# A new opening list for an attention-and-gate kernel; two lower parts of U are made by TensorE and ScalarE

## The chip, the cores and the metric

The kernel runs on one core of a Trainium2 chip. The metric is device time in microseconds (us), lower is better: the median of three runs, and one profiled execution that shows where the time goes.

The core has five engines that work side by side, each through its own instructions in order: TensorE (PE; its weight loads, PEld, are listed apart), VectorE (DVE), ScalarE (ACT), GpSimd (POOL) and SyncE (SP), which here issues most of the DMA transfers. Matrix products go to PSUM, which has eight banks.

## The reference

```python
a = exp(phi - max(phi, axis=2))                    # phi: 8 batches, 8 heads, 576 rows, 32 memories
a = a / (sum(a, axis=2) + 1e-9)
k_m = einsum('bhsm,bhsd->bhmd', a, k)              # d = 64
v_m = einsum('bhsm,bhsd->bhmd', a, v)
s = q @ k_m.T / 8
attn = exp(s - max(s)); attn = attn / (sum(attn) + 1e-9)
x = (attn @ v_m)                                   # to 4608 tokens x 512
gate = sigmoid(x @ w_gate); val = x @ w_val        # 512 x 1536 each
out = (gate * val) @ w_out                         # 1536 x 512
```

The gate weights and the output weights arrive as 64-bit floats and are made into 32-bit ones by integer operations in the kernel.

## The kernel before

Products that must be exact to about 32 bits are made of three products in a rounded format: every operand is split into an upper part (hi, a rounded copy, made by ScalarE) and a lower part (lo, the rest, a subtraction on VectorE by `rest`, L150). x is never formed: U = v_m x [w_gate, w_val] is made for each batch and each pair of the 12 column tiles f, and then attention (`at`) times U gives gate and value at once.

The work goes in steps (batch b, tile f), 96 in all. The first four batches go through f 0 to 3, then 4 to 7, then 8 to 11; the others through all twelve at a time. A step has two halves c (256 and 320 tokens). A half is: 12 products into one or two banks (`G`), sigmoid on ScalarE (`sg`), product on VectorE (`gm`), hi on ScalarE (`gh`), lo on VectorE (`gl`), and some halves later six products with the output weights (`O`). Beside these run the attention pieces of later batches and the conversion of weights (`CONVERT`: at which step which piece).

The first eight steps, and all loads and preparations ahead of them, are written out by hand in a list, `OPENING`, a word for each piece of work. Each word is recorded in turn, and each of the engines PE, DVE, ACT and POOL keeps the list's order; the transfers keep their order on the queue that issues them. The words that matter here:

- loads (all on SP's queue): `phi b`, `kvm b g` and `kvt b` (keys and values), `q b c`, `gate f` (gate weights of tile f, into the wg area that tiles 4 to 11 will fill later), `out f` (output weights); `more`: the next weights of the conversion table, on POOL's queue before;
- batch b's memories: `amax`, `aexp` (exponential of phi), `T`, `A`, `Z` (turn by TensorE, copy, sum), `K`, `B`, `t`, `V` (keys and values, copies and turns);
- batch b's attention, in halves for b 0: `S` (scores), `tr` (VectorE turns them), `mx`, `ex`, `nm` (softmax), `tn` (turn back), `hi`, `lo` (the two parts of `at`). For b 1 and 2 `tn` writes into the tile named q, which the next batch's q needs;
- weights: `sz` and `bt` (magnitude on ScalarE, four operations on VectorE) for a gate piece; `ws`, `wb`, `wh`, `wl` for output weights;
- `U b f` (eight 32-bit products into two banks, which the trace shows as 16 rows), `uh`, `ul` (hi and lo);
- `E` (the sums of a finished turn, copied to a row and sent away), `W n`: n products on the identity that nothing reads.

`turn_lo` also sends both parts of `at` to memory, for use in later turns, as soon as they are there.

Of the kernel before, what the change touches and what calls it, by code (L numbers as in the profile page):

```python
# [54 lines left out]
A 0 1; q 0 0; sz 2; q 0 1; A 0 0; W 23; K 0 0; bt 2; sz 1; bt 1; W 28; K 0 1; B 0; kvt 1; kvm 1 0;  # L55
kvm 1 1; amax 1; W 5; t 0; V 0 0; V 0 1; W 2; S 0 0; aexp 1; U 0 0; tr 0 0; mx 0 0; S 0 1; uh 0 0;
T 1 1; T 1 0; Z 1; A 1 1; T 1 2; ul 0 0; phi 2; A 1 0; q 1 0; A 1 2; out 3; ex 0 0; tr 0 1; q 1 1; W 7;
K 1 0; out 2; nm 0 0; kvm 2 0; mx 0 1; W 8; K 1 1; B 1; kvm 2 1; tn 0 0; kvt 2; amax 2; ex 0 1; W 5;
t 1; hi 0 0; V 1 0; nm 0 1; aexp 2; W 6; S 1 0; V 1 1; W 5; T 2 2; lo 0 0; T 2 1; A 2 2; S 1 1; tn 0 1;
A 2 1; G 0 0 0; Z 2; hi 0 1; tr 1 0; lo 0 1; T 2 0; tr 1 1; U 0 2; sg 0 0 0; mx 1; A 2 0; G 0 0 1;  # L60
uh 0 2; sg 0 0 1; G 0 1 0; gm 0 0 1; gm 0 0 0; ul 0 2; K 2 0; ex 1; G 0 1 1; gh 0 0 0; nm 1; K 2 1;
sg 0 1 0; gh 0 0 1; G 0 2 0; B 2; kvt 3; out 1; gm 0 1 0; gl 0 0 0; gh 0 1 0; U 1 0; gl 0 0 1;
sg 0 1 1; gl 0 1 0; sg 0 2 0; gm 0 1 1; G 0 2 1; uh 1 0; gm 0 2 0; tn 1; gh 0 1 1; t 2; sg 0 2 1;
ul 1 0; G 0 3 0; hi 1; gm 0 2 1; V 2 0; O 0 0 0; lo 1; ws 1; V 2 1; G 0 3 1; gl 0 1 1; q 2 1; gh 0 2 0;
wb 1; phi 3; sg 0 3 0; kvm 3 0; q 2 0; O 0 0 1; gl 0 2 0; wh 1; gm 0 3 0; G 1 0 0; sg 0 3 1; wl 1;
gh 0 2 1; gm 0 3 1; ws 2; gl 0 2 1; O 0 1 0; sg 1 0 0; wb 2; more; G 1 0 1; gh 0 3 0; gm 1 0 0; wh 2;
gl 0 3 0; amax 3; U 1 2; sg 1 0 1; O 0 1 1; uh 1 2; wl 2; gm 1 0 1; ws 3; ul 1 2; S 2 0; O 0 2 0;
tr 2 0; aexp 3; wb 3; S 2 1; G 1 1 0; gh 0 3 1; tr 2 1; gh 1 0 0; O 0 2 1; wh 3; gl 0 3 1; gl 1 0 0;
# [9 lines left out]
def attn_moe_kernel(  # L78
# [97 lines left out]
    def words_tile(room):  # L176

        if len(wos) == 1:
            return pools["conv"].tile([P, 512, 2], I32, name="words", bufs=room)
        if not late_words:  # L180
            q = att([P, NKT * S], "q").bitcast(I32)
            late_words.append(pools["conv"].tile([P, 512, 2], I32, name="words"))
            late_words.extend(q[:, o : o + 1024].rearrange("p (n t) -> p n t", t=2) for o in (0, 1024))
        late_words.append(late_words.pop(0))
        return late_words[-1]
# [820 lines left out]
```

## Time and profile before

| | |
|---|---|
| median of three runs | 754.13 us (752.48 to 754.15) |
| profiled execution | 754.74 us, span 753.0 us |
| instructions | 13818 |
| busy, PE / PEld / DVE / ACT / POOL | 729.6 / 609.9 / 432.4 / 337.7 / 13.7 us |
| moved by DMA | 93.17 MB |

The span is the time from the first to the last instruction of the program; some two microseconds of the execution lie around it. A line of the timeline names start, length, engine, line, operation, output and inputs, shapes, and in brackets the engine's idle time before it and what ended that. "PE busy" counts the W products too, so that the opening looks fuller than it is.

### The profile page before, as it was taken

The numbers are of one execution on the slowest core, as the hardware profiler recorded it, in microseconds if no ns is written. First come the engines' busy times: TensorE is split into PE (matmuls) and PEld (weight loads), VectorE is DVE, ScalarE is ACT, GpSimd is POOL, SyncE is SP. The second block draws the span as 40 slices with busy tenths as digits, with TensorE's granted clock in tenths as the row PEclk, the third lists the DMA queues.
The fourth block names the chain that finished last, engine by engine and source line by source line (L and its number), as shares of the span: only waits on it lengthen the run. The fifth ranks groups of instructions, "written<-read, shape, count | busy, mean of one in ns | idle before, by whom it ended". The sixth has DMA issues, their size and how long they took to land.

```text
span 753.0 us, 13818 instructions
## 1 busy us (share of the span) xinstructions
PE 729.6 (97%) x5651; PEld 609.9 (81%) x5651; DVE 432.4 (57%) x824; ACT 337.7 (45%) x784; POOL 13.7 (2%) x30
## 2 busy tenths in 40 slices
PE   7998999989999999999999999999999999999997
PEld 5676787868889888878888798887887888888886
DVE  7898656986678854447537634356245643343332
ACT  4387545647444433335434443355333533343331
POOL 0000000011000000000000000000000000000000
PEclk9899899999999999999999999999999999999999
DMA  9977255658557544432344104011000000010002
GB/s 360 360 301 286 86 210 186 232 191 295 188 188 246 182 143 146 161 124 66 134 136 163 64 1 172 1 57 64 2 2 29 29 1 15 1 57 1 1 1 70
DMA packets 30655, 93.17 MB, mean 124 GB/s; under 512 B 3456, under 2 KB 4480, under 8 KB 28032
## 3 DMA queue, kind: packets, MB, share of 16 engines
q1 hardware_dynamic: 22528, 71.31, 26.2%
q0 software_dynamic: 3456, 12.58, 5.0%
q10 hardware_dynamic: 4608, 8.39, 3.3%
q8 instruction: 44, 0.72, 0.4%
q14 instruction: 19, 0.16, 0.1%
HBM read 69.73 MB, written 22.54 MB: 123 GB/s over the span
## 4 chain that ended last, share of the span: by engine, by line
PE 87%; DMA 5%; DVE 4%; ACT 2%; issue 1%; SPq 1%; ACTq 0%; DVEq 0%
PE pu_t L160 52%; PE acc L160 36%; DMA kvm<-in_kvm_dram 2%; DMA q<-in_qT_dram 2%; DMA words<-in_wgv_dram 1%; SPq L146 1%; DMA out_dram<-row 1%; ACT L135 1%; ACT ph L135 0%; ACT sg L135 0%; DVE u_lo L150 0%; ACT at_hi L523 0%; DVE g_lo L150 0%; DVE wg L248 0%; DVE at_lo L150 0%
## 5 line engine op out<-in xcount | busy, mean ns | idle before, releaser
L160 PE MATMUL pu_t<-at_hi,u_hi 128*128 128x256 f32 (+1 forms) x760 | 226.9, 299 | 1.1 <-ACT sg L135 1.1
L160 PE MATMUL pu_t<-at_lo,u_hi 128*128 128x256 f32 (+1 forms) x760 | 223.3, 294 | 0.0
L160 PE MATMUL pu_t<-at_hi,u_lo 128*128 128x256 f32 (+1 forms) x760 | 223.0, 293 | 0.0
L638 DVE TENSOR_TENSOR sg<-pu_t,sg 128x256 f32<-128x256 f32 (+1 forms) x190 | 86.3, 455 | 171.7 <-ACT sg L135 106.5
L135 ACT ACTIVATE sg<-pu_t 128x256 f32<-128x256 f32 (+1 forms) x190 | 78.2, 412 | 188.3 <-PE pu_t L160 180.7
L160 PE MATMUL acc<-wo_hi,g_hi 128*128 128x512 f32 x384 | 154.7, 403 | 0.0
L160 PE MATMUL acc<-wo_hi,g_lo 128*128 128x512 f32 x384 | 151.5, 394 | 0.0
L160 PEld LDWEIGHTS pu_t<-at_hi,u_hi 128*128 128x128 f32 x760 | 142.8, 188 | 10.5 <-issue 2.4
L160 PE MATMUL acc<-wo_lo,g_hi 128*128 128x512 f32 x384 | 151.1, 394 | 0.0
L160 PEld LDWEIGHTS pu_t<-at_lo,u_hi 128*128 128x128 f32 x760 | 142.8, 188 | 5.3
L160 PEld LDWEIGHTS pu_t<-at_hi,u_lo 128*128 128x128 f32 x760 | 142.6, 188 | 0.0
L649 ACT CAST g_hi<-sg 128x256 fp32r<-128x256 f32 x192 | 77.9, 406 | 113.1 <-DVE sg L638 101.8
L150 DVE TENSOR_TENSOR g_lo<-sg,g_hi 128x256 fp32r<-128x256 f32 x192 | 80.4, 420 | 58.2 <-ACT g_hi L649 58.2
L160 PEld LDWEIGHTS acc<-wo_hi,g_hi 128*128 128x128 f32 x384 | 72.2, 188 | 30.7 <-issue 20.9
L160 PEld LDWEIGHTS acc<-wo_hi,g_lo 128*128 128x128 f32 x384 | 72.4, 189 | 17.2
L160 PEld LDWEIGHTS acc<-wo_lo,g_hi 128*128 128x128 f32 x384 | 72.4, 188 | 9.6
L150 DVE TENSOR_TENSOR u_lo<-pu_t,u_hi 128x512 fp32r<-128x512 f32 x93 | 58.3, 683 | 24.7 <-ACT u_hi L569 24.6
L569 ACT CAST u_hi<-pu_t 128x512 fp32r<-128x512 f32 x93 | 48.1, 598 | 27.1 <-PE pu_t L160 27.0
L160 PE MATMUL pu_t<-wg,vT 64*32 64x512 f32 x744 | 49.3, 596 | 3.1 <-DVE wg L248 2.3
L160 PEld LDWEIGHTS pu_t<-wg,vT 64*32 64x32 f32 x744 | 11.4, 105 | 26.0 <-issue 16.6
L135 ACT ACT_TABLE_LOAD x20 | 25.7, 1283 | 2.8 <-DVE g_lo L150 1.8
L689 DVE TENSOR_TENSOR row<-acc,row 128x512 f32<-128x512 f32 x32 | 22.0, 688 | 5.5 <-DMA row<-part 5.5
(110 smaller groups left out, 587.5 us busy)
## 6 DMA issues: line engine op xcount, KB each, us to landing
kvm<-in_kvm_dram SPq DMA_DIRECT2D x16, 1024.0 KB, 8.8
q<-in_qT_dram SPq DMA_DIRECT2D x16, 512.0 KB, 5.4
part<-row SPq DMA_DIRECT2D x32, 256.0 KB, 2.1
row<-part ACTq DMA_DIRECT2D x32, 256.0 KB, 4.5
out_dram<-row SPq DMA_DIRECT2D x32, 256.0 KB, 2.1
words<-in_wgv_dram POOLq DMA_DIRECT2D x10, 512.0 KB, 4.6
ph<-in_phiT_dram SPq DMA_DIRECT2D x8, 576.0 KB, 5.1
at_hi<-at SPq DMA_DIRECT2D x8, 576.0 KB, 4.6
```

Source lines behind the costliest of these rows:

```text
L135: last_act[0] = nc.scalar.activation(*args, **kw)
L146: last_move[queue] = queues[queue].dma_start(dst, src)
L150: return nc.vector.tensor_tensor(lo, x, hi.bitcast(F32), op=ALU.subtract)
L160: last_pe[0] = do(*args, **kw)
L569: nc.scalar.copy(U[b, fs[0]][0][:, r, :nf], pb[r])
L638: last_prod[0] = nc.vector.tensor_tensor(sg, val, sg, op=ALU.mult)
L649: nc.scalar.copy(ghi, prod[:, : 2 * P])
L689: nc.vector.tensor_tensor(st, o, st, op=ALU.add)
```

## The change

The whole opening list is new, and with it some pieces of work are cut more finely or given to another engine:

- Gates 2, 1 and 0 are loaded first, in that order, then converted; gate 3 and all output weights come much later. There are 103 W products in place of 155.
- `bt` is cut in two words (`bc` clamps, `bt` sets the bits), likewise `wb` (`wc`, `wb`), `mx` (`mx`, `ms`) and `nm` (`nz`, `nm`).
- For U 0 0 and U 0 2 the lower part is no longer a subtraction on VectorE. A matrix `minus` (the identity times -1) is multiplied with hi into the same two banks, the eight products of U are added once more (`um`), and ScalarE copies what remains (`u_rest`).
- U 2 2 moves from the tenth step into the list.
- `at` of batches 0 to 2 is sent away by words of their own (`keep`), and the finished rows too (`row`); copies of finished sums of batches 0 to 3 are all ScalarE's (half were VectorE's).
- Gate pieces of the conversion table are 1024 columns wide (512 before), at most two pieces wait at a time, `more` uses SP's queue, and the first conversion comes at step 9 in place of 10. `normalize` and `turn` of later batches are recorded behind the gate work, and the slots in which pieces of later batches come are other ones.

```diff
-out 0; phi 0; gate 0; gate 3; gate 2; kvm 0 0; kvt 0; gate 1; kvm 0 1; ws 0; wb 0; amax 0; wh 0; wl 0;
-sz 0 0; sz 0 1; bt 0 0; aexp 0; bt 0 1; sz 3; W 42; T 0 0; T 0 2; T 0 1; Z 0; A 0 2; bt 3; phi 1;
...
+kvt 0; gate 2; phi 0; gate 1; kvm 0 0; gate 0; kvm 0 1; sz 2; bc 2; amax 0; bt 2; sz 1; aexp 0; bc 1;
+bt 1; W 56; T 0 2; T 0 0; A 0 2; T 0 1; A 0 0; phi 1; sz 0 1; K 0 0; q 0 0; A 0 1; bc 0 1; q 0 1;
+sz 0 0; kvm 1 0; Z 0; bc 0 0; W 3; K 0 1; bt 0 1; B 0; kvt 1; kvm 1 1; amax 1; W 5; t 0; V 0 0; bt 0 0;
...
-    10: [(4, 0)], 11: [(4, 1)], 12: [(5, 0), (5, 1)], 13: [(6, 0), (6, 1)], 14: [(4, 2), (7, 0)], 15: [(7, 1), (5, 2)],
+    9: [(4, 0)], 10: [(5, 0)], 12: [(6, 0)], 13: [(4, 2)], 14: [(7, 0)], 15: [(5, 2)], 16: [(6, 2)], 18: [(7, 2)],
...
+BY_PE = [(0, 0), (0, 2)]
...
-        halves_of[b] = halves_of.get(b, 0) + (2 if c is None else 1)
-        if b < QUAD and halves_of[b] == 2:
-            kept[b] = [dram.tile([P, 2 * S], F32, name=f"at{b}_{i}") for i in range(2)]
-            for d, a in zip(kept[b], at[b]):
-                move(d, a.rearrange("p r n -> p (r n)").bitcast(F32))
+        if QUAD > b >= 3:
+            put_by(b)
...
+    def u_minus(b, fs):
+        pb, hi = loaded[b, "u", fs[0]], U[b, fs[0]][0]
+        for r in range(2):
+            matmul(pb[r], minus, hi[:, r, : len(fs)], start=True, stop=False)
+        u_sum(b, fs, pb, False)
+    def u_rest(b, fs):
+        pb, nf = loaded.pop((b, "u", fs[0])), len(fs)
+        hi, lo = U[b, fs[0]]
+        for r in range(2):
+            last_u[0] = nc.scalar.copy(lo[:, r, :nf], pb[r])
...
-            elif t % 2:
+            elif t % 2 or b < QUAD:
                 nc.scalar.copy(st, o)
...
+    minus = pools["conv"].tile([P, P], F32R, name="minus", bufs=1)
+    nc.scalar.activation(minus, ident, AF.Copy, scale=-1.0)
...
-        begin[2, 0]: ([3, 3, 2, 2, 2, 1], remember(3, True), score(3), attend(3)),
-        begin[0, TURN]: ([2, 2, 1, 1, 1, 1, 1], remember(4)),
+        begin[2, 0]: ([3, 2, 2, 2, 2, 1, 1], remember(3, True), score(3), attend(3)),
+        begin[0, TURN]: ([2, 1, 1, 1, 1, 1, 1, 1], remember(4)),
...
-        sides[begin[b, 0]] = ([1] * 23, score(b + 1, then), attend(b + 1))
+        sides[begin[b, 0]] = (([1] * 6 + [0] * 2) * 3, score(b + 1, then), attend(b + 1))
...
-        if i == DONE + 1:
-            make_u(b, [2, 3])
```

How the rows of the built program move, at three places. First the head of SP's queue, the transfers that everything waits for at the start (words: output weights; wg: gate weights; ph: phi). Before:

```order
L146 DMA words<-in_wo_dram 128x1024
L146 DMA ph<-in_phiT_dram 128x1152
L146 DMA wg<-in_wgv_dram 128x2048 x3
L146 DMA kvm_126<-in_kvm_dram 128x2048
L146 DMA kvt<-in_kvt_dram 128x512
L146 DMA wg<-in_wgv_dram 128x2048
L146 DMA kvm_131<-in_kvm_dram 128x2048
L146 DMA ph<-in_phiT_dram 128x1152
L146 DMA q<-in_qT_dram 128x1024 x2
L146 DMA q<-in_qT_dram 128x256
```

Now:

```order
L146 DMA kvt<-in_kvt_dram 128x512
L146 DMA wg<-in_wgv_dram 128x2048
L146 DMA ph<-in_phiT_dram 128x1152
L146 DMA wg<-in_wgv_dram 128x2048
L146 DMA kvm_127<-in_kvm_dram 128x2048
L146 DMA wg<-in_wgv_dram 128x2048
L146 DMA kvm_130<-in_kvm_dram 128x2048
L146 DMA ph<-in_phiT_dram 128x1152
L146 DMA q<-in_qT_dram 128x1024 x2
L146 DMA q<-in_qT_dram 128x256
```

The output weights are gone from the head, three gates stand there in place of four, and kvt is first.

Second, VectorE from the lower part of batch 0's first half of `at` (at_lo from u_hi, which serves as a room for the turn there) on. Before, the second half's turn and batch 1's scores follow, and then the softmax of batch 1 and the first gate products:

```order
L150 TENSOR_TENSOR at_lo<-u_hi,at_hi 128x2x256
L516 STREAM_TRANSPOSE u_lo<-e 128x320 x2
L364 TENSOR_SCALAR z<-z 128x2
L365 RECIPROCAL rz<-z 128x2
L467 STREAM_TRANSPOSE e<-pu_t 128x256 x2
L150 TENSOR_TENSOR at_lo<-u_lo,at_hi 128x2x320
L467 STREAM_TRANSPOSE e<-acc_577 128x320
L467 STREAM_TRANSPOSE e<-pu_t 128x320
L476 TENSOR_REDUCE mx<-e 128x36
L477 TENSOR_TENSOR e<-e,mx 128x1152
L638 TENSOR_TENSOR sg<-acc_653,sg 128x320
L638 TENSOR_TENSOR sg<-pu_t,sg 128x256
```

Now batch 1's scores come at once, the gate products are mixed with the conversion of gate 3 (wg, 1024 columns):

```order
L150 TENSOR_TENSOR at_lo<-u_hi,at_hi 128x2x256
L478 STREAM_TRANSPOSE e<-acc_509 128x256
L478 STREAM_TRANSPOSE e<-acc_510 128x256
L150 TENSOR_TENSOR at_lo<-u_lo,at_hi 128x2x320
L478 STREAM_TRANSPOSE e<-acc_527 128x320
L478 STREAM_TRANSPOSE e<-pu_t 128x320
L246 TENSOR_SCALAR wg<-wg 128x1024
L247 TENSOR_SCALAR wg<-wg 128x1024
L682 TENSOR_TENSOR sg<-pu_t,sg 128x256
L254 SCALAR_TENSOR_TENSOR wg<-wg 128x1024
L257 SCALAR_TENSOR_TENSOR wg<-wg 128x1024
L682 TENSOR_TENSOR sg<-acc_581,sg 128x320
```

The turn and the sums of phi stand ahead of this piece now, and gate 3's four operations have come into it; the softmax of batch 1 is further down.

Third, SP's queue around the loads of batch 2's q and batch 3's phi. Before (the first row is batch 0's `at` going out, the next at rows batch 1's; q 2 1 comes in two pieces, q 2 0 is the last row):

```order
L146 DMA at_1_620<-at_lo 128x1152
L146 DMA kvt<-in_kvt_dram 128x512
L146 DMA words<-in_wo_dram 128x1024
L146 DMA at_0_858<-at_hi 128x1152
L146 DMA at_1_859<-at_lo 128x1152
L146 DMA q<-in_qT_dram 128x1024
L146 DMA q<-in_qT_dram 128x256
L146 DMA ph<-in_phiT_dram 128x1152
L146 DMA kvm_894<-in_kvm_dram 128x2048
L146 DMA q<-in_qT_dram 128x1024
```

Now (q 2 0 is the fourth row, q 2 1 the two after the gate words):

```order
L146 DMA kvm_690<-in_kvm_dram 128x2048
L146 DMA at_0_694<-at_hi 128x1152
L146 DMA at_1_695<-at_lo 128x1152
L146 DMA q<-in_qT_dram 128x1024
L146 DMA words<-in_wo_dram 128x1024
L146 DMA ph<-in_phiT_dram 128x1152
L146 DMA words<-in_wgv_dram 128x2048
L146 DMA q<-in_qT_dram 128x1024
L146 DMA q<-in_qT_dram 128x256
L146 DMA kvm_949<-in_kvm_dram 128x2048
```

q 2 0 goes ahead of out 3, phi 3 and the gate words, q 2 1 behind them; batch 1's `at` is further down.

More of the change, by code (lines that the diff above doesn't have):

```diff
@@ L54 @@
-sz 0 0; sz 0 1; bt 0 0; aexp 0; bt 0 1; sz 3; W 42; T 0 0; T 0 2; T 0 1; Z 0; A 0 2; bt 3; phi 1;
[L55 to L68, printed above, removed]
@@ new lines @@
+bt 1; W 56; T 0 2; T 0 0; A 0 2; T 0 1; A 0 0; phi 1; sz 0 1; K 0 0; q 0 0; A 0 1; bc 0 1; q 0 1;
+sz 0 0; kvm 1 0; Z 0; bc 0 0; W 3; K 0 1; bt 0 1; B 0; kvt 1; kvm 1 1; amax 1; W 5; t 0; V 0 0; bt 0 0;
+V 0 1; W 2; S 0 0; aexp 1; S 0 1; tr 0 0; U 0 0; mx 0 0; tr 0 1; T 1 1; uh 0 0; T 1 2; T 1 0; ms 0 0;
+phi 2; A 1 0; um 0 0; Z 1; q 1 1; ex 0 0; mx 0 1; A 1 2; nz 0 0; A 1 1; K 1 0; ul 0 0; ms 0 1; K 1 1;
+nm 0 0; ex 0 1; amax 2; B 1; kvt 2; q 1 0; nz 0 1; W 5; t 1; gate 3; aexp 2; kvm 2 1; out 0; tn 0 0;
@@ new lines @@
+nz 1; O 0 0 0; sg 0 2 1; V 2 1; gm 0 2 1; O 0 0 1; sg 0 3 0; nm 1; gh 0 2 0; wh 1; G 0 3 1; gh 0 2 1;
+gl 0 2 0; wl 1; tn 1; ws 2; O 0 1 0; sg 0 3 1; gm 0 3 0; hi 1; gm 0 3 1; U 1 2; wc 2; gh 0 3 0;
+O 0 1 1; lo 1; uh 1 2; ul 1 2; G 1 0 0; q 2 0; gh 0 3 1; out 3; phi 3; gl 0 3 0; more 0; wb 2; G 1 0 1;
+q 2 1; kvm 3 1; gl 0 3 1; wh 2; gl 0 2 1; G 1 1 0; wl 2; sg 1 0 0; sg 1 0 1; gm 1 0 0; ws 3; gm 1 0 1;
+O 0 2 0; sg 1 1 0; wc 3; gm 1 1 0; wb 3; G 1 1 1; gh 1 0 0; gl 1 0 0; wh 3; amax 3; S 2 0; sg 1 1 1;
@@ new lines @@
+O 0 2 1; gm 1 1 1; tr 2 0; S 2 1; wl 3; aexp 3; U 2 0; tr 2 1; O 0 3 0; mx 2; uh 2 0; G 1 2 0;
+gh 1 0 1; ms 2; E 0 3 0 0; gh 1 1 0; row 0 0; O 0 3 1; ul 2 0; E 0 3 0 1; ex 2; row 0 1; gl 1 1 0;
+G 1 2 1; gl 1 0 1; gh 1 1 1; nz 2; E 0 3 1 0; E 0 3 1 1; O 1 0 0; row 1 1; gl 1 1 1; kvt 3; nm 2;
+G 1 3 0; sg 1 2 0; sg 1 2 1; gm 1 2 0; gm 1 2 1; O 1 0 1; gh 1 2 0; tn 2; sg 1 3 0; G 1 3 1; gh 1 2 1;
+gm 1 3 0; gl 1 2 0; hi 2; gl 1 2 1; O 1 1 0; sg 1 3 1; lo 2; U 2 2; gm 1 3 1; gh 1 3 0; q 3 1;
+gl 1 3 0; keep 1; O 1 1 1; more 1; uh 2 2; row 1 0; q 3 0; ul 2 2; keep 2; gh 1 3 1; O 1 2 0; gl 1 3 1;
@@ L174, in attn_moe_kernel, with words_tile @@
     late_words = []
-    def words_tile(room):
+    def words_tile(k):
         if len(wos) == 1:
[L179 to L185, printed above, removed]
+            words = pools["conv"].tile([P, 1024, 2], I32, name="words", bufs=2)
+        elif k == 2:
+            words = pools["conv"].tile([P, 512, 2], I32, name="words")
+        else:
+            if not late_words:
+                late_words.append(att([P, NKT * S], "q").bitcast(I32)[:, :2048].rearrange("p (n t) -> p n t", t=2))
+            words = late_words[0]
+        return words[:, :512] if k == 2 else words
     def load_jobs(n=None, queue="stream"):
@@ L199, in load_jobs @@
             n = n and n - 1
+    early_out = []
     def load_out(f):
-        words = words_tile(WORDS[0])
+        if not early_out:
+            early_out.extend(pools["conv"].tile([P, 1024, 2], I32, name="words", bufs=2) for _ in range(2))
+        words = words_of[f, 2] = early_out[f // 2][:, f % 2 * 512 : f % 2 * 512 + 512]
         move(words.rearrange("p n t -> p (n t)"), wo[f].bitcast(I32))
-        words_of[f, 2] = words
-        waiting.append((f, 2))
     def target(f, k):
@@ L244, in bits_of @@
         )
+    def bits_of(dst, words):
+        low, high, bits = words[:, :, 0], words[:, :, 1], dst.bitcast(I32)
         nc.vector.scalar_tensor_tensor(
@@ L694, in out_end, with out_put @@
                 nc.vector.tensor_copy(st, o)
-            if f == NFT - 1:
-                move(out[b * S + t * P : b * S + (t + 1) * P, :], st)
-            else:
-                part[b, t] = dram.tile([P, DM], F32, name=f"part{b}_{t}_{f}")
-                move(part[b, t], st)
+            stored[b, t] = st
+            if put:
+                out_put(b, f, t)
+    stored = {}
+    def out_put(b, f, t):
+        st = stored.pop((b, t))
+        if f == NFT - 1:
+            move(out[b * S + t * P : b * S + (t + 1) * P, :], st)
+        else:
+            part[b, t] = dram.tile([P, DM], F32, name=f"part{b}_{t}_{f}")
+            move(part[b, t], st)
     rows = {}
@@ L856, in attend @@
     def attend(b):
-        normalize(b)
+        with behind():
+            normalize(b)
         yield
-        turn(b)
+        with behind():
+            turn(b)
         if b + 1 < B and b + 1 != QUAD:
```

78 lines of the change are left out of this document (51 added, 27 removed), and 3 rows, old and new, of the table CONVERT.

## The prediction, made before the changed kernel was run

> **What bounds the kernel now.** I read the busy shares first, then what TensorE waits for, then the busy times stage by stage, then the start of the trace in order of time.
>
> ```profile
> PE 729.6 (97%) x5651; PEld 609.9 (81%) x5651; DVE 432.4 (57%) x824; ACT 337.7 (45%) x784; POOL 13.7 (2%) x30
> ...
> PE pu_t L160 <- DMA q<-in_qT_dram: 4.2, 1, 4.2
> ...
> PE pu_t L160 <- DVE wg L248: 2.3, 2, 1.8
> PE pu_t L160 <- ACT ph L135: 1.8, 1, 1.8
> ```
>
> TensorE is busy 97% of the span, so time can only come from where it is idle, or busy with nothing. Its longest waits are a load of q, one of keys and values (4.0, its row is below), two on converted gate weights, one on an exponential. The stages show the rest (columns: length; busy us of PE, weight loads, DVE, ACT, POOL; granted clock; DMA share; GB/s):
>
> ```profile
> 0.00:29.89 29.89, 24.24 (x241) 18.84 (x249) 21.55 (x31) 12.50 (x23) 1.37 (x7) 0.89 0.90 351
> 29.89:42.91 13.02, 11.53 (x225) 8.10 (x210) 12.67 (x26) 9.00 (x24) 0.00 (x0) 1.00 1.01 400
> 42.91:71.97 29.06, 29.06 (x291) 23.95 (x280) 27.61 (x50) 21.24 (x43) 1.06 (x2) 1.00 0.74 275
> 71.97:82.06 10.09, 5.89 (x57) 3.49 (x58) 4.01 (x11) 4.52 (x10) 0.53 (x1) 0.66 0.24 92
> 103.55:200.00 96.45, 91.33 (x782) 74.73 (x781) 70.32 (x138) 54.12 (x122) 7.07 (x13) 1.00 0.66 230
> ```
>
> Up to 29.89 (VectorE's first transpose of scores) TensorE's busy time is mostly idle products on the identity that the list calls W; the DMA engines are at work 90% of it. From 29.89 to 42.91 (first gate product, G 0 0 0) VectorE is busy 12.67 of 13.02 us: it sets the pace. From 42.91 TensorE is gapless until it runs into the q load at 71.97. So the opening list ends at 103.71, where the first gate of the ninth step starts, and from there 754.74 - 103.71 = 651.03 us are left (754.74 is the profiled execution's own time; the median of the runs is 754.13, 0.6 lower).
>
> **Term 1: the first score transpose, 29.89 before.** The DMA queue is a queue in order: what stands ahead in it comes first. Landings show as the ends of waits:
>
> ```profile
> 8.26 1.25 ACT L227 ACTIVATE wg<-wg 128x512 f32<-128x512 f32 x2 [0.23 <-DMA wg<-in_wgv_dram]
> 13.60 1.17 ACT L227 ACTIVATE wg<-wg 128x1024 f32<-128x1024 f32 x1 [0.41 <-DMA wg<-in_wgv_dram]
> 18.95 1.94 PE L160 MATMUL pu_t<-kvm,e 128*32 128x128 f32 x32 [4.00 <-DMA kvm<-in_kvm_dram]
> 25.75 1.08 PE L160 MATMUL pu_t<-kvm,e 128*32 128x128 f32 x32
> ...
> kvm<-in_kvm_dram SPq DMA_DIRECT2D x16, 1024.0 KB, 8.8
> ph<-in_phiT_dram SPq DMA_DIRECT2D x8, 576.0 KB, 5.1
> wg<-in_wgv_dram SPq DMA_DIRECT2D x4, 1024.0 KB, 9.8
> words<-in_wo_dram SPq DMA_DIRECT2D x4, 512.0 KB, 5.3
> kvt<-in_kvt_dram SPq DMA_DIRECT2D x8, 256.0 KB, 4.1
> ```
>
> Two gate pieces land in 13.60 - 8.26 = 5.3 us; I take 2.5 us per 1024 KB, since instruction fetches and a words load share the engines there. Before, 512 + 576 + 1024 KB were in at 8.2. Now kvt and gate 2 come first, 832 KB less: 8.2 - 2.0 = 6.2. Then phi 7.6, gate 1 10.1, kvm 12.6, gate 0 15.1, the second kvm 17.6, phi 1 19.0, q 0 until 21.8. The second half of the keys, before at 25.75 behind 28 idle products, can run at 17.6; from it to the first transpose it took 29.89 - 25.75 = 4.1, so scores are there at about 21.8.
>
> VectorE, though, has three gate pieces to convert ahead of its first transpose:
>
> ```profile
> L227 ACT ACTIVATE wg<-wg 128x1024 f32<-128x1024 f32 x3 | 3.5, 1152 | 7.2 <-DMA wg<-in_wgv_dram 7.2
> L242 DVE TENSOR_SCALAR wg<-wg 128x1024 int32<-128x1024 int32 x3 | 2.1, 693 | 0.1
> L245 DVE SCALAR_TENSOR_TENSOR wg<-wg 128x1024 int32<-128x1024 int32 x3 | 3.7, 1226 | 0.1
> L322 DVE TENSOR_REDUCE nmx<-ph 128x2 f32<-128x1152 f32 x5 | 6.7, 1341 | 1.1 <-DMA ph<-in_phiT_dram 1.1
> L322 DVE TENSOR_REDUCE nmx<-ph 128x1 f32<-128x576 f32 x2 | 1.4, 744 | 0.0
> L241 DVE TENSOR_SCALAR wg<-wg 128x512 f32<-128x512 f32 x11 | 4.6, 420 | 0.3
> L245 DVE SCALAR_TENSOR_TENSOR wg<-wg 128x512 int32<-128x512 int32 x2 | 1.4, 692 | 0.1
> ```
>
> It starts at 6.2 + 1.15 (the magnitude on ScalarE) = 7.4. Gates 2 and 1: 2 x (2 x 0.69 + 2 x 1.226) = 7.7. Gate 0 in halves: 4 x 0.42 + 4 x 0.692 = 4.45. The maxima of phi: 2 x 0.744 + 1.341 = 2.83; two small ones 0.3. Sum 15.2 us, each piece landed before its turn (gate 0 by 15.8, phi 1 by 19.0). That ends at 22.6; means overlap by a twentieth where VectorE runs without a gap (between the next two rows their sum is 13.2, the time 12.5), so 21.9 to 22.6: **22.3**, 7.6 earlier than 29.89. Before, gate 3 and out 0 were converted ahead too (3.8 + 2.9 us). They are not gone, but moved behind.
>
> **Term 2: to lo 1, the lower part of batch 1's attention, which G 1 0 0 needs.**
>
> ```profile
> 29.89 0.78 DVE L467 STREAM_TRANSPOSE e<-acc 128x256 f32<-128x256 f32 x2 [1.56 <-PE acc L160]
> 41.72 0.69 DVE L150 TENSOR_TENSOR at_lo<-u_hi,at_hi 128x512 fp32r<-128x512 f32 x1
> 59.50 1.36 DVE L150 TENSOR_TENSOR at_lo<-q,at_hi 128x1152 fp32r<-128x1152 f32 x1 [0.27 <-ACT at_hi L523]
> ...
> L150 DVE TENSOR_TENSOR u_lo<-pu_t,u_hi 128x512 fp32r<-128x512 f32 x19 | 12.4, 681 | 2.2 <-ACT u_hi L569 2.1
> L638 DVE TENSOR_TENSOR sg<-pu_t,sg 128x320 f32<-128x320 f32 x19 | 9.2, 486 | 4.1 <-PE pu_t L160 3.9
> L638 DVE TENSOR_TENSOR sg<-pu_t,sg 128x256 f32<-128x256 f32 x19 | 8.0, 419 | 12.9 <-ACT sg L135 12.9
> L150 DVE TENSOR_TENSOR g_lo<-sg,g_hi 128x256 fp32r<-128x256 f32 x40 | 16.3, 416 | 5.3 <-ACT g_hi L649 5.3
> ```
>
> From the first transpose to lo 0 0 took 41.72 + 0.69 - 29.89 = 12.5. The new list takes out U 0 0's two lower parts (2 x 0.68, now TensorE's and ScalarE's) and puts in the second turn of e (0.98) and two small ones (0.33): the same, 12.5. G 0 0 0 then stands at 34.8, 8.1 earlier than 42.91.
>
> From lo 0 0 to lo 1 took 59.50 + 1.36 - 42.41 = 18.45. Out of that stretch: the turn and the small ones, -1.3; U 0 2's lower parts, -1.4. Into it: gate 3, +3.8; out 0 and out 1 (2 x 0.42 + 2 x 0.69 + 0.68 each), +5.8; the clamp of out 2, +0.85; two more products and two more lower parts of g, +1.75. That makes 28.0, so lo 1 ends at 62.8, **later** than its 60.86 before. TensorE does more ahead of it, however: besides the first batch's four gates the list puts U 1 2, both halves of O 0 1 and the identity's products before G 1 0 0. That work is 25.6 us by the rows below, so TensorE arrives at 60.4 and waits 2.4 in all.
>
> **Term 3: from G 1 0 0 to the end of the list.**
>
> ```profile
> 254.09 4.59 PE pu_t L160 x36
> ...
> 100.95 2.76 PE acc L160 x12
> ...
> 249.24 1.88 PE pu_t L160 x32
> ...
> 30.38 0.75 PE L160 MATMUL pu_t<-q,kT 64*32 64x256 f32 x32
> ```
>
> Three gate halves (short, long, short) take 4.59, so a short and a long one 3.17; two halves of O 2.76; two U 1.88; the long part of a set of scores 0.75, the short no more. The list has four such gate pairs (12.7), nine halves of O (12.4), S 2 (1.4), U 2 0 and U 2 2 (1.9): 28.4. VectorE's queue has 26.7 us by means until lo 2, which the next step's gate needs: under TensorE's.
>
> What goes is the q wait. Before, q 2 0 stood behind the other part of q, phi 3 and a kvm in the queue:
>
> ```profile
> 63.71 12.32 DMA q<-in_qT_dram
> ...
> 17.20:24.05 6.85, 5.10 (x54) 3.93 (x55) 5.34 (x7) 1.12 (x1) 0.00 (x0) 0.50 1.01 423
> 75.20:82.06 6.86, 5.89 (x57) 3.49 (x58) 3.56 (x10) 1.32 (x3) 0.53 (x1) 0.50 0.02 7
> ```
>
> It cost 4.2 of idle time and, since the clock stood at 0.50 for the next 6.86, some 2.9 more for 5.89 of work. Now q 2 0 goes first once lo 1 frees its tile (62.8): in by 66. Out 3, phi 3, 1024 KB of gate words and q 2 1 (640 KB) follow on the same queue: in by about 73. S 2 stands nine microseconds of TensorE work behind G 1 0 0, at 72: late next is q 2 1, by one at most. Taking 2 us for that and for waits that nothing here shows, the list ends at 22.3 + 12.5 + 28.0 + 28.4 + 2.0 = **93.2** in place of 103.71.
>
> **The identity.**
>
> ```profile
> L569 ACT CAST u_hi<-pu_t 128x512 fp32r<-128x512 f32 x93 | 48.1, 598 | 27.1 <-PE pu_t L160 27.0
> ```
>
> U 0 0 and U 0 2 each gain two products of 512 columns and a second set of eight: at 0.23 apart (12 in 2.76) and 0.94 it is 1.4 us of TensorE each, all counted above. A product with the -1 matrix has no row; at twice that spacing it would be 1.9, and zero is the other end, where TensorE waits for VectorE anyway. ScalarE takes 4 x 0.60 (as for u_hi), beside other work: it was busy 21.24 of 29.06. Cover for that: VectorE's queue. If that ran early, the 2.8 would be bare.
>
> **After the list.** U 2 2 (0.94) is no longer in the ninth step. The gate conversions are whole pieces (3.8 in place of 2 x 2.2, eight times), the first ones one or two steps earlier; six row copies of batches 1 to 3 go from VectorE to ScalarE; phi 4 is turned a slot later after its exponential. So the 2.3 us that U for gates 4 to 7 waits on wg go, and I count 1.2 of the 1.8 on phi: -3.5; ends 0 and, with other gaps, -5.5. The reordered pieces of later batches I take at nothing, covered by VectorE's slack there. Sum: 93.2 + 651.03 - 0.94 - 3.5 = 739.8, against the profiled 754.74; against the median some 739.2. I forecast **740**.
>
> **The clock, by a rule.** Idle times of 4.0 and 4.2 us were each followed by 6.85 us at 0.50; 1.8 us was not. The Trainium skill ("TensorE: Matmul & The Clock Gate", Part 1: The HAM clock gate) says that the rate halves after an idle window of about 3.4 us that runs freely of the kernel. The rows agree as far as they go. My 2.4 us before G 1 0 0 lies between the two cases; by the row nearest to it (1.8) nothing happens.
>
> **Rivals.**
> - VectorE's queue has gaps. Each landing or ScalarE result that comes late shifts everything behind it, since the sums leave no room. For it: in the first 29.89 it idled 8.3. Against: 27.61 of 29.06 busy later. The first transpose at 25 (+2.7), 3 more of waits, and half of the later gain lost: 747.
> - The wait before G 1 0 0 grows over 3.4 us in one piece, and the clock halves: 6.85 us at half cost 3.4, so 743. One microsecond of slip in VectorE is enough, but only if no U or O falls into it.
> - Given back: from 103.55 to 200 VectorE runs 70.32 of 96.45, most of it before 170. If the gate conversions set the end of that stretch whatever the opening, the list's 10.5 and the later 3.5 both go: 754.
> - Slower: ScalarE becomes the bound of the list. By means it has 48 us of work in the 58 from G 0 0 0 to the end, in order, with three results per gate half that VectorE waits for. It decides when each of the 16 halves loses 0.9 us: 14.9 is gone, and at 1.1 the time is 757. Against: it is busy 21.24 of 29.06 at present, and each of its results stands ahead of its use by a microsecond in my walk through the two queues.
>
> **How the numbers follow.** Forecast (736 to 744) 0.57; gaps 0.19; half clock 0.11; given back 0.05; slower 0.05; better than 736 0.03. Under 0.3% (2.3 us) nothing can be told from no change. Given back counts as the same four times in five: faster 0.91, same 0.04, slower 0.05. The range goes from all small gains (739.2 - 2 - 2 = 735) to the gaps with the wait before U 1 2 grown as well (750).
>
> **What would show it.** Right: first score transpose near 22, first gate product near 35, lo 1 near 63, no wait on q over 1 us, clock 1.00 past 30, first gate of batch 2 near 93. Wrong: VectorE idle over 3 us between 8 and 63; a PE wait over 3.4; a wait on wg still in the list of waits.

## The result, and the profile after

The changed kernel takes 747.28 us (median of four runs, 744.57 to 748.77) beside 754.14 for the kernel before on the same chip: ratio 0.9898 [0.9871, 0.9925]. On a second chip (the run e5_after below) it is 747.24 beside 754.52, ratio 0.9905 [0.9884, 0.9926]. The profiled execution shown here took 748.77, with a span of 746.9. Of the five runs of e10 below two took 1709 and 2492 us, and its ratio leaves them out.

The page's busy times and the list of what TensorE waits for (us in all, times, longest):

```profile
PE 724.1 (97%) x5635; PEld 606.2 (81%) x5635; DVE 420.0 (56%) x780; ACT 338.2 (45%) x787; POOL 8.3 (1%) x20
```

```profile
PE pu_t L160 <- DMA kvm<-in_kvm_dram: 2.9, 1, 2.9
PE pu_t L160 <- ACT kT L424: 2.6, 1, 2.6
PE pu_t L160 <- ACT sg L135: 2.0, 2, 1.2
PE pu_t L160 <- DVE wg L257: 1.8, 1, 1.8
PE acc L160 <- DVE row L733: 1.5, 2, 1.1
...
PE acc L160 <- DMA q<-in_qT_dram: 1.0, 1, 1.0
...
PE pu_t L160 <- DMA q<-in_qT_dram: 1.0, 1, 1.0
```

The 4.2 us on q 2 0 are gone; the last line is 0.97 us on q 2 1, at 77 us, and the other line on q is batch 1's, at 36. The two waits on wg after the list are gone; the wg line that is left is gate 3, inside the list. In second and fifth place stand waits that the kernel before had only at 0.2 us each, or not at all. The stages, cut at the same events as before (first score transpose, first gate product, G 1 0 0, first gate of batch 2):

```profile
0.00:25.15 25.15, 19.50 (x214) 15.12 (x221) 14.80 (x23) 10.90 (x22) 0.70 (x6) 0.86 0.94 381
25.15:37.77 12.62, 11.40 (x229) 7.71 (x214) 12.08 (x28) 10.46 (x25) 0.00 (x0) 1.00 0.82 294
37.77:65.83 28.06, 26.24 (x274) 20.92 (x272) 25.50 (x43) 21.81 (x44) 0.00 (x0) 1.00 0.57 214
65.83:96.40 30.57, 29.60 (x231) 24.06 (x230) 26.55 (x49) 18.70 (x40) 0.00 (x0) 1.00 0.54 196
96.40:746.86 650.46, 637.36 (x4708) 538.36 (x4706) 341.08 (x640) 276.30 (x658) 7.65 (x14) 1.00 0.30 104
```

For the last one, the stage from the first gate of batch 2 to the end, the kernel before has

```profile
103.55:753.00 649.45, 637.42 (x4724) 537.20 (x4722) 349.40 (x680) 276.71 (x662) 10.77 (x20) 1.00 0.29 101
```

So the whole gain of this execution is in the list (96.40 in place of 103.55, 7.15 us); the 88 steps after it take 1.0 us longer than before, with TensorE as busy (637.36 beside 637.42) and idle 13.1 us in place of 12.0. The waits there were not removed but exchanged. That stage differs from execution to execution, however. Counted up to the execution's full time it is 652.4 us here and 651.7, 651.0, 649.7 and 647.9 in e5, e8, e3 and e4 below, which have the same code there; the kernel before has 651.2, and 653.1 in e6. On average that is 1.6 us less than before.

Where the list lost against the forecast is its start. TensorE's row for the second half of batch 0's keys, VectorE's first transpose, and three windows of TensorE around them (the last number but two is the clock):

```profile
19.02 1.93 PE L160 MATMUL pu_t<-kvm,e 128*32 128x128 f32 x32 [2.92 <-DMA kvm<-in_kvm_dram]
...
25.15 0.78 DVE L478 STREAM_TRANSPOSE e<-acc 128x256 f32<-128x256 f32 x2 [2.15 <-PE acc L160]
```

```profile
14.84:18.25 3.41, 1.27 (x35) 0.77 (x26) 3.27 (x9) 1.74 (x3) 0.00 (x0) 1.00 1.00 404
18.25:21.66 3.41, 2.64 (x42) 2.22 (x43) 2.56 (x4) 0.17 (x1) 0.00 (x0) 0.50 1.06 427
21.66:25.08 3.42, 3.38 (x35) 2.12 (x40) 1.31 (x3) 2.30 (x7) 0.00 (x0) 0.50 1.02 422
```

TensorE stands 2.92 us until the keys are there; then the clock is at 0.50 until 25.08, just while the keys' second half, the turns and the first scores run, for which VectorE waits 2.15 us.

### The profile page after: what moved, and what is told of

The parts are those of the page before. It is cut to its first block, busy times and chain, and to the rows that moved or that the text cites. A ratio compares the mean times of both kernels' runs of the same rounds, so it can differ in the third digit from the quotient of the medians.

```text
span 746.9 us, 13717 instructions
## 1 busy us (share of the span) xinstructions
PE 724.1 (97%) x5635; PEld 606.2 (81%) x5635; DVE 420.0 (56%) x780; ACT 338.2 (45%) x787; POOL 8.3 (1%) x20
## 4 chain that ended last, share of the span: by engine, by line
PE 83%; DMA 8%; DVE 4%; ACT 2%; issue 1%; SPq 1%; ACTq 0%; DVEq 0%
PE pu_t L160 50%; PE acc L160 33%; DMA kvm<-in_kvm_dram 2%; DMA part<-row 2%; DMA row<-part 1%; DMA q<-in_qT_dram 1%; DMA wg<-in_wgv_dram 1%; SPq L146 1%; DMA ph<-in_phiT_dram 1%; DVE u_lo L150 1%; DMA out_dram<-row 1%; ACT L135 1%; DVE sg L682 0%; DVE row L733 0%; ACT row L736 0%
## 5 line engine op out<-in xcount | busy, mean ns | idle before, releaser
L160 PEld LDWEIGHTS pu_t<-at_hi,u_hi 128*128 128x128 f32 x756 | 142.6, 189 | 13.1 <-issue 3.0
L150 DVE TENSOR_TENSOR u_lo<-pu_t,u_hi 128x512 fp32r<-128x512 f32 x90 | 56.1, 682 | 24.5 <-ACT u_hi L598 24.5
```

Of the source, the lines that this page charges most:

```text
L150: return nc.vector.tensor_tensor(lo, x, hi.bitcast(F32), op=ALU.subtract)
L160: last_pe[0] = do(*args, **kw)
```

## The experiments

Four ran on one chip beside the kernel before (754.42), four on a second (754.52), three on a third (753.27), one on a fourth (755.2). Each is compared with the kernel before on its own chip. "After" is the changed kernel.

**e1_queue.** The last finished row of batch 0 (`row 1 0`), batch 1's `at` (`keep 1`) and the second gate words (`more 1`) go out directly behind `row 1 1`:

```
 ... O 1 0 0; row 1 1; +row 1 0; keep 1; more 1;+ gl 1 1 1; kvt 3; ...
 gl 1 3 0; -keep 1;- O 1 1 1; -more 1;- uh 2 2; -row 1 0;- q 3 0; ...
```

> The changed kernel with three words of the list moved ahead in the DMA queue: the last row of batch 0, batch 1's attention parts and the second gate words go out before batch 2's finished attention is waited for. Queue theory (after the list, row copies on ScalarE wait for a row's transfer that stands behind 2.3 MB of attention parts and 1 MB of words; the copy of batch 3's keys stands behind them, and with it batch 3's scores and first gate): the wait of 2.6 us on the keys' copy near 109 and most of the 2.4 us near 126 to 137 go, with the half clock after it: 4 to 6 us less than the changed kernel, ratio to the kernel before 0.982 to 0.985. Rival (batch 3's attention is late because it is recorded behind the gate work and a slot later): at most 1 us less, ratio 0.988 to 0.991, the wait near 135 stays.

745.0 us (742.84 to 745.31), ratio 0.9864 [0.9843, 0.9885]: 2.3 us less than after, with intervals that overlap by little. ScalarE's rows at that place, of after and of this kernel:

```profile
104.06 0.59 ACT L736 COPY row<-acc 128x512 f32<-128x512 f32 x1 [0.28 <-DMA part<-row]
...
110.16 0.59 ACT L736 COPY row<-acc 128x512 f32<-128x512 f32 x1 [1.29 <-DMA part<-row]
...
111.43 0.39 ACT L424 COPY kT<-pu_t 128x256 f32<-128x256 f32 x1
```

```profile
103.75 1.07 ACT L736 COPY row<-acc 128x512 f32<-128x512 f32 x2
...
109.31 0.58 ACT L736 COPY row<-acc 128x512 f32<-128x512 f32 x1
110.08 0.60 ACT L736 COPY row<-acc 128x512 f32<-128x512 f32 x1
110.56 0.39 ACT L424 COPY kT<-pu_t 128x256 f32<-128x256 f32 x1
```

In after the row copies wait for the store of an earlier row (there are two row tiles), and the copy of batch 3's keys, kT, which TensorE needs, is queued behind them. With the three transfers issued earlier these waits go, and TensorE's wait on kT is 1.2 us in place of 2.6. Over the runs this wait follows that of the third row copy: 2.6, 2.5, 2.5, 2.3 and 1.9 us where that is 1.29, 1.20, 1.19, 0.94 and 0.58 (after, e7, e8, e5, e3), and 1.2 to 1.3 where there is none (e1, e9, and also e4, whose queue is not changed). So the edit is worth some 1.4 us here. The rest of the queue theory did not come true: the waits on batch 3's attention near 135 us stay (0.58 and 1.01). From the first gate of batch 2 on this execution takes 745.31 - 96.94 = 648.4, which lies inside the 647.9 to 652.4 of the five executions with after's code there, so the difference to after's 652.4 shows nothing by itself.

**e2_attend.** The softmax sums and the turn of the attention pieces are no longer put behind VectorE's other work:

```
-        with behind():
-            normalize(b)
+        normalize(b)
         yield
-        with behind():
-            turn(b)
+        turn(b)
...
-        begin[2, 0]: ([3, 2, 2, 2, 2, 1, 1], remember(3, True), score(3), attend(3)),
+        begin[2, 0]: ([3, 3, 2, 2, 2, 1], remember(3, True), score(3), attend(3)),
```

> The changed kernel with the later batches' normalize and turn no longer recorded behind the gate work, and the old slots (3, 3, 2, 2, 2, 1) beside batch 2's steps. Attend theory: the waits on batch 3's attention near 126 to 137 (2.4 us and 1.7 us of half clock) go, 3 to 4 us less than the changed kernel, ratio 0.985. Queue theory: the copy of batch 3's keys stays late whatever the slots, 1 us less at most, or more time since a score's transpose stands ahead of a gate product: ratio 0.988 to 0.992.

749.37 us (746.76 to 750.57), ratio 0.9924 [0.9902, 0.9947]: no gain. Around 132 us TensorE waits 1.3 and 1.5 us on the two parts of batch 3's attention, where after waits 0.6 and 1.0. Recording these pieces earlier, with the old slots, does not make them ready earlier.

**e3_warm.** TensorE is kept at work while the second keys are under way:

```
- ... Z 0; bc 0 0; W 3; K 0 1; bt 0 1; ...
+ ... Z 0; bc 0 0; W 30; K 0 1; bt 0 1; ...
```

> The changed kernel with 30 idle products in place of 3 ahead of the second half of batch 0's keys, which fill the 2.9 us in which TensorE waits for kvm. Clock theory (that wait lets the clock fall to 0.50 from 18.25 to 25.08, the keys, turn and scores run at half speed, and VectorE's first transpose waits 2.15 us for them): the first transpose comes at 23.0 to 23.5 instead of 25.15, no half clock before 30, and the whole is 1.5 to 2 us less, ratio 0.987. Rival (the transfers that follow set the pace, so VectorE waits for phi and gate 3 a little later): the first transpose is earlier but lo 1 still ends near 66, ratio 0.989 to 0.991.

743.82 us (742.18 to 744.75), ratio 0.9854 [0.9831, 0.9878]. No half clock at the start; first score transpose at 23.21, first gate of batch 2 at 93.71. VectorE's row:

```profile
23.21 0.78 DVE L478 STREAM_TRANSPOSE e<-acc 128x256 f32<-128x256 f32 x2 [0.34 <-PE acc L160]
```

Its wait for the scores is 0.34 in place of 2.15. Twenty-seven products that nothing reads make the kernel 3.4 us faster, more than the 1.5 to 2 expected: the first gate of batch 2 comes 2.7 us earlier than in after and 2.1 earlier than in e5_after, and the rest, after the list, no run takes apart. That the clock is what costs, and not the gap itself, e2 shows. There TensorE waits for the same keys, but no half clock follows:

```profile
18.92 1.08 PE L160 MATMUL pu_t<-kvm,e 128*32 128x128 f32 x32 [2.67 <-DMA kvm<-in_kvm_dram]
...
23.05 0.78 DVE L478 STREAM_TRANSPOSE e<-acc 128x256 f32<-128x256 f32 x2
```

From the keys' second half to the first transpose it takes 4.1 us there, as the prediction had it, and 6.1 in after (19.02 to 25.15).

**e4_noident.** The four lower parts of U go back to VectorE:

```
-BY_PE = [(0, 0), (0, 2)]
+BY_PE = []
...  (um 0 0 and um 0 2 leave the list)
```

> The changed kernel without the identity: the lower parts of U 0 0 and U 0 2 are VectorE's subtraction again, the 2.8 us of products on TensorE and the four copies on ScalarE are gone. If VectorE's queue sets the pace up to lo 1, as the prediction had it, lo 1 ends 2.7 us later (68.6) and the whole is 2 to 2.7 us longer than the changed kernel, ratio 0.993. If TensorE or the transfers set it, the whole is 0 to 2.8 us shorter, ratio 0.986 to 0.990.

745.09 us (743.93 to 745.57), ratio 0.987 [0.9848, 0.9892]: lo 1 ends at 66.58 (after 65.95), the first gate of batch 2 stands at 97.15 (96.40), and the time is no higher than after's. Its half clock at the start lasted 3.41 us, though, after's 6.83. The executions with the identity whose half clock there was as long (e1, e5, e7) have lo 1 at 65.0 to 66.1 and the first gate at 95.8 to 96.9, so without it both come 0.2 to 1.5 us later, not 2.7. The time does not show it: after the list, where the code is the same, this execution was the shortest of the five (647.9).

**e5_after.** The changed kernel once more.

> The changed kernel itself, once more, beside the three that follow on this chip. Median 745 to 748, ratio 0.987 to 0.993. The profile of before had one idle stretch of 2.9 us at 16 us followed by 6.83 us at half clock; if the length of the half clock is a matter of chance, this profile shows the same idle stretch with another length (0, 3.4 or 6.8), and the first score transpose moves with it between 23 and 25 us. If it belongs to the kernel, it is 6.8 again.

("The profile of before" is here the changed kernel's first profile, the one shown above.) 747.24 us (745.34 to 749.13), ratio 0.9905 [0.9884, 0.9926]. The idle time at 16 us is the same, 2.87, but the half clock behind it is 3.41 us long and not 6.83; two more stretches of 3.41 follow at 36 and 111 us. The first transpose stands at 24.26.

**e6_before_q.** The kernel before, with one load moved:

```
- ... gl 0 1 1; q 2 1; gh 0 2 0; wb 1; phi 3; sg 0 3 0; kvm 3 0; q 2 0; ...
+ ... gl 0 1 1; q 2 0; q 2 1; gh 0 2 0; wb 1; phi 3; sg 0 3 0; kvm 3 0; ...
```

> The kernel before, with only the load q 2 0 moved ahead of q 2 1, phi 3 and the keys of batch 3. Theory: the wait on q (4.2 us) and the half clock behind it (2.9) were a cost of their own, which one move in the list takes away: 754 - 7 = 747, or 749 if a wait of 2 us on something else takes its place; first gate of batch 2 at 97 to 99 in place of 103.6. Rival: the load was late only because TensorE was ahead of VectorE there, so another wait of the same length stands in its place: 752 to 754.

749.65 us (747.7 to 751.93), ratio 0.9934 [0.9911, 0.9956]: 4.9 us from one word of the list. The first gate of batch 2 stands at 98.84. In place of the 4.2 us on q TensorE waits 1.44 us ahead of the same scores of batch 2, now on a gate product of VectorE's (the last line), and the clock stays up there; the waits on the keys (4.5) and on wg are as before:

```profile
PE pu_t L160 <- DMA kvm<-in_kvm_dram: 4.5, 1, 4.5
PE pu_t L160 <- DVE wg L248: 2.3, 2, 1.8
PE pu_t L160 <- ACT ph L135: 2.2, 2, 1.8
PE pu_t L160 <- DVE sg L638: 1.9, 2, 1.4
```

The size is that of the second of the two expected times. About two thirds of what the change gives can be had without the new list.

**e7_amax.** The maximum of phi 4 put behind VectorE's other work of its step:

```
-            a_max(b)
+            with behind():
+                a_max(b)
```

> The changed kernel, with the maximum of phi 4 put behind VectorE's other work of that step instead of ahead of batch 3's score transposes. Theory: that maximum waits 1.96 us for its load at 117 us and holds batch 3's attention behind it, so that TensorE waits at 126, 135 and 136 us (2.4 us in all, and half clock once). Then these waits fall under 0.8 us in all and the time by 1.5 to 3 us against the changed kernel. Rival: batch 3's attention is late because the copy of its scores on ScalarE is late (the wait of 2.6 us at 109); then the waits at 126 to 137 stay, and the time is the same within 1 us.

749.76 us (747.7 to 751.37), ratio 0.993 [0.9908, 0.9952]: the theory fell. The wait at 126 us, which is one on a sigmoid, went; those on batch 3's attention stayed (0.4 and 1.0), and the exponential of phi 4 now came too late for its turn, at 168.9:

```profile
PE pu_t L160 <- ACT ph L135: 3.7, 2, 3.4
```

**e8_qgate.** q 1 0 and gate 3 loaded ahead of kvt 2:

```
- amax 2; B 1; kvt 2; q 1 0; nz 0 1; W 5; t 1; gate 3; aexp 2;
+ amax 2; q 1 0; gate 3; B 1; kvt 2; nz 0 1; W 5; t 1; aexp 2;
```

> The changed kernel, with the loads q 1 0 and gate 3 put ahead of kvt 2, whose issue waits for TensorE's last product on batch 1's keys. Theory: that wait holds the DMA queue from 27.9 to 31.7 us, so that gate 3 lands at 40.3 and VectorE waits 2 us for it, and S 1 waits 1 to 2.4 us for q 1 0. Then both waits are gone, lo 1 ends 1.5 to 2 us earlier, at about 64, and the time falls by 1 to 2 us. Rival: VectorE's queue has other work late there (batch 1's scores); lo 1 stays at 66 and the time is the same within 1 us.

744.52 us (742.95 to 745.87), ratio 0.9865 [0.9845, 0.9886], 2.7 less than after on the same chip. VectorE's row for gate 3 in after, and SyncE's queue in after and here:

```profile
41.53 0.69 DVE L246 TENSOR_SCALAR wg<-wg 128x1024 f32<-128x1024 f32 x1 [1.97 <-ACT wg L229]
```

```profile
28.33 0.85 SPq L146 DMA_DIRECT2D q<-in_qT_dram  x2
31.73 0.33 SPq L146 DMA_DIRECT2D kvt<-in_kvt_dram  x1
32.10 0.42 SPq L146 DMA_DIRECT2D q<-in_qT_dram  x1
32.58 1.05 SPq L146 DMA_DIRECT2D wg<-in_wgv_dram  x1
```

```profile
26.79 1.84 SPq L146 DMA_DIRECT2D q<-in_qT_dram  x2
28.67 0.44 SPq L146 DMA_DIRECT2D wg<-in_wgv_dram  x1
30.46 0.33 SPq L146 DMA_DIRECT2D kvt<-in_kvt_dram  x1
```

Gate 3 is issued 3.9 us earlier. From the first transpose to lo 1 it takes 62.71 - 22.99 = 39.7 us, after 65.95 - 25.15 = 40.8, and e5_after as much: the move gives 1.1 us there. TensorE's wait on gate 3 falls from 1.8 to 0.3, and the one on q of batch 1 (1.0 at 36 us) goes. The profiled execution also had its second keys earlier (a wait of 1.53 us), no half clock at the start and its first transpose at 22.99; why the start went better than in e5_after the runs do not show.

**e9_three.** The edits of e1, e3 and e8 together.

> The changed kernel with three edits of the list at once: 30 idle products in place of 3 ahead of K 0 1; rows 0 of the first batch put by directly behind rows 1; q 1 0 and gate 3 loaded ahead of kvt 2. Alone they gave -3.4, -2.3 and -2.7 us against 747.2. If they act on different waits, 747.2 - 8.4 = 739; if the first and the third share the half clock at 18 to 25 us (1.7 us on average, since its length is 0 to 6.8 us), 740 to 741. First score transpose at 23, lo 1 at 62.5, first gate of batch 2 at 92.5. Rival: what is won at the start is given back by the waits at 130 to 200: 743.

741.19 us (740.11 to 743.82), ratio 0.9836 [0.9811, 0.9862]. First transpose 23.24, lo 1 63.20, first gate of batch 2 92.53; no half clock at all until the tail. They add up as far as the second case, 740 to 741.

**e10_three_noident.** That kernel without the identity, as in e4.

> The kernel with the three edits, without the identity: the first batch's four lower parts of U go back to VectorE. The prediction's step: TensorE's 2.8 us are covered only as long as VectorE is late, and VectorE is spared 4 x 0.68 = 2.7 us; then lo 1 and the first gate of batch 2 come 1.5 to 2.7 us later without it, and the time rises as much. Rival: VectorE's queue loses nothing by these four, since it waits there for scores or loads anyway; the first gate of batch 2 moves by under 0.8 us, TensorE does 2.8 us less, and the time is the same or up to 1 us lower.

744.81 us, ratio 0.9872 [0.9843, 0.99], from three executions of 743.89 to 744.81 us beside 740.11 to 743.82 for e9 on the same chip. All three are longer than each of e9's five, though the intervals of the ratios overlap, so the identity seems worth some 3 us here. Where is less clear. The first gate of batch 2 stands at 94.21, 1.7 later than in e9; but the three executions that have the three edits and the identity (e9, e11, e12) differ among themselves, with lo 1 at 62.2 to 64.2 (63.78 here) and the first gate at 91.5 to 93.9. Another 1.7 us of the difference to e9's profile is half clock (3.41 us at 133), behind the same waits that no half clock followed in e9.

**e11_three_rows.** The three edits, and the reloads of partial rows issued by SyncE:

```
-            move(st, part[b, t], "rows")
+            move(st, part[b, t])
```

> The kernel with the three edits, with the reloads of the partial rows (row from part) issued by SyncE instead of ScalarE. Theory: ScalarE stands in front of such a reload until the store of the same row (part from row, or the output from row) has landed, 3.9 to 5.5 us at 195 to 201 us and 2 us at 395, where gate words of 1024 KB, put on the stream queue in one piece by the change, are under way in the same DMA engines; everything queued behind it on ScalarE, sigmoids above all, is late, and TensorE waits 1.4 to 2.2 us at 197 to 199 and 1.1 at 397. Then ScalarE's waits for part from row outside the list (7 us) go, TensorE's waits at 197 to 206 and at 397 too, and the time falls by 2 to 3 us against the three edits alone. Rival: the reload is as late on SyncE, and TensorE waits for the row itself (sum of the accumulators); same within 1 us.

771.69 us (769.61 to 771.86), ratio 1.0225 [1.0201, 1.0249]. ScalarE's waits for part from row (13.5 us in e9) did go, but TensorE waits

```profile
PE acc L160 <- DVE row L733: 21.0, 9, 6.9
```

that is, 21.0 us in all in place of 0.8 in e9. On SyncE a reload stands in one queue with the stores of the rows, which wait for VectorE's sums, which wait for the reload ahead:

```profile
381.91 0.43 SPq L146 DMA_DIRECT2D row<-part  x1
387.27 0.34 SPq L146 DMA_DIRECT2D out_dram<-row  x1
387.71 0.59 SPq L146 DMA_DIRECT2D row<-part  x1
```

```profile
386.55 0.69 DVE L733 TENSOR_TENSOR row<-acc,row 128x512 f32<-128x512 f32 x1 [3.81 <-DMA row<-part]
390.80 0.69 DVE L733 TENSOR_TENSOR row<-acc,row 128x512 f32<-128x512 f32 x1 [3.56 <-DMA row<-part]
```

Each row is loaded back only once the one ahead of it is summed and stored. ScalarE's waits before the reloads were the cheaper ones.

**e12_three_rowcopy.** The three edits, and half of the row copies of batches 1 to 3 back on VectorE:

```
-            elif t % 2 or b < QUAD:
+            elif t % 2:
```

> The kernel with the three edits (741.19 us, ratio 0.9836), with half of the row copies of batches 1 to 3 given back from ScalarE to VectorE, as the kernel before had it. Theory: the row copies on ScalarE cost nothing where VectorE is late and hold the keys' copy (kT) where ScalarE is; in the list they are the ones that TensorE's wait of 1.2 us at 105 stands behind. With half of them on VectorE this wait falls under 0.7, and the time by 0.5 to 1.5 us: ratio 0.982 to 0.983. Rival: VectorE is the later of the two there, as the prediction's walk through its queue had it; its copies hold the products of the gates and batch 3's attention, whose waits at 129 to 131 us (1.6 in all) grow by 1 to 2 us: ratio 0.985 to 0.987.

740.65 us (738.25 to 744.07), ratio 0.9803 [0.977, 0.9836]. The wait on kT falls from 1.2 to 0.7 as expected. The ratio is lower than e9's 0.9836 [0.9811, 0.9862], but on another chip and with intervals that overlap: which of the two is better is not settled. Both beat the kernel before and the changed one. The filling of the gap has a price of its own here: batch 0's first keys ran later than in e9 (15.37 beside 14.32), the thirty idle products pushed the second ones to 19.98, and the first transpose stands at 24.12 without any half clock.

## Why the prediction came out as it did, step by step

The time, 740 forecast and 747.3 measured, lies inside the range and on the side forecast, but the forecast's own band (736 to 744) missed it. The sum against the profiled execution, 748.77, was 9.0 too low. The sum also read the end of the list before as 103.71, where the first gate of batch 2 stands at 103.55, and called the step that U 2 2 leaves the ninth, which is the tenth; neither changes the sum by more than 0.2. By its terms, in us:

| term | forecast | measured | difference |
|---|---|---|---|
| 1: first score transpose | 22.3 | 25.15 | +2.85 |
| 2: from there to lo 1 | 40.5 | 40.80 | +0.3 |
| 3: lo 1 to first gate of batch 2 | 30.4 | 30.45 | +0.05 |
| after the list | 646.6 | 652.4 | +5.8 |

These are one execution's. The first and the last term vary with the clock and with waits: over the executions with the same code up to there or from there on (after, e1, e2, e4, e5 and e7; after, e3, e4, e5 and e8) the first transpose lay between 23.05 and 25.15, and the last term between 647.9 and 652.4, never at its forecast.

**Term 1: the step that failed** is "The second half of the keys ... can run at 17.6; from it to the first transpose it took ... 4.1". It asked when the load would be in and not what TensorE would do until then. The three gates landed as the sum had them (ScalarE starts on them at 6.14, 10.07 and 15.05), the second keys 1.4 us later (19.02; 17.75 in e8); why, no run shows. The change cut the idle products ahead of K 0 1 from 28 to 3, so TensorE had nothing to do for 2.92 us, and the clock fell for the very products that the first transpose waits for: 6.1 us in place of 4.1. The prediction weighed that danger ahead of G 1 0 0, where nothing came of it (G 1 0 0 stood at 65.83, without a wait), and not here. e3 takes the gap away: 23.21, and 3.4 us of time. Of the 0.9 that stays against 22.3, 0.60 is VectorE's wait for phi 1, which the sum had landing in time, and 0.34 its wait for the scores.

**Term 2** held as a number: 12.5 forecast to lo 0 0, 12.2 measured (25.15 to 37.33); 28.0 forecast on to lo 1, 28.6 measured. That lo 1 would come later than before, in spite of a start that is earlier, was right as well (65.95 beside 60.85). But the second stretch is not 28 us of work without a gap:

```profile
37.33:65.95 28.62, 26.80 (x289) 21.33 (x275) 26.06 (x46) 22.18 (x45) 0.00 (x0) 1.00 0.57 216
```

VectorE is busy 26.06 us of it and idle 2.56, of which 1.97 is the wait for gate 3 (e8). The sum took means end to end, without the overlap that term 1 had allowed for, and no idle time. That the two errors nearly cancel is luck.

**Term 3** held, with the parts a little different: 29.6 us of TensorE's work in place of 28.4, 1.0 of waits in place of 2.0. The wait on q 2 0 and the half clock behind it went, as said; the wait on q 2 1 was 0.97, with "one at most" forecast. e6 shows that the wait on q 2 0 and its half clock were a term of their own, 4.9 of the 7.1 counted.

**The identity**: TensorE's price was 1.4 us each between 0 and 1.9; the two products with the -1 matrix are 0.75 together,

```profile
27.57 0.76 PE L160 MATMUL pu_t<-u_hi,minus 128*128 128x512 f32 x2
```

so with 0.94 for the repeated eight 1.7. ScalarE's copies are 585 ns, as taken. Its worth, forecast at 2.7 us of VectorE's queue, was 0.2 to 1.5 at the first gate of batch 2 in e4 and 0.3 to 2.7 in e10, by the execution that is set beside it; the time shows it in e10 alone.

**After the list: the second step that failed.** The waits on wg (2.3) and on phi (1.8) did go from there; what failed is "The reordered pieces of later batches I take at nothing, covered by VectorE's slack there". New waits stand in the place of the old ones: 2.6 on kT at 109, 0.8 on a sigmoid at 126, 1.6 on the two parts of batch 3's attention at 135 and 136 with half clock behind them (3.41 us long, 1.7 of cost), 1.5 on row sums at 206 and 234, 1.2 on a sigmoid at 398. For the first, two causes are shown, both in ScalarE's queue: row copies that wait for a store (1.4 of the 2.6, by e1 and the rows of seven other runs) and, of the 1.2 that stays, half a microsecond for the number of row copies ahead (e12). For batch 3's attention a cause is only argued: VectorE has no slack there at all. Its busy time (the third figure after the length) from the end of the wait at 126 to the end of the one at 136, in after, and over the twelve microseconds ahead of phi 4:

```profile
100.00:112.00 12.00, 9.37 (x132) 8.10 (x138) 3.64 (x7) 7.47 (x18) 0.00 (x0) 1.00 0.76 292
...
127.16:137.23 10.07, 8.50 (x57) 4.86 (x57) 10.02 (x16) 5.61 (x14) 0.53 (x1) 1.00 0.21 76
```

It is busy 10.02 of 10.07 us, and the edits of e2, e7 and e12 on VectorE left 1.4 to 2.8 us of these waits. What should help is to start batch 3's scores earlier, where VectorE does 3.64 us of work in 12; that was not tried. For the waits behind 200 us, ScalarE stands before a reload until the store of an earlier row has landed, as in after:

```profile
201.21 0.41 ACT L693 CAST g_hi<-sg 128x256 fp32r<-128x256 f32 x1 [3.85 <-DMA part<-row]
```

That TensorE waits because of it is only argued, since e11, which was to show it, put larger waits in their place.

**The rivals.** "VectorE's queue has gaps" came nearest (747), and with the first transpose at 25 even at the place. It was right that there are gaps: VectorE is busy 48.64 of the 55.00 us from 8 to 63 in after, so the 3 us of idle time named as a sign of being wrong was passed, at 6.4. But the largest gap was made by TensorE's clock, and the ones between 25 and 66 were made up for by the overlap. Of the other signs of being wrong one came as well, a wait on wg in the list (gate 3). The half clock ahead of G 1 0 0 did not happen, nor did given back, nor ScalarE as the bound: the list kept 7.15 of its forecast 10.5, and ScalarE's waits decided only single places.
